# One core, two branches (dilated attention and a long convolution): even and odd tokens instead of mirrored ones, partner frequencies by adding DMAs, and an order written by a planner

## The chip, the cores and the metric

The kernel runs on one core of a Trainium2 chip. Its engines are TensorE (PE, with a queue of weight loads, PEld), VectorE (DVE), ScalarE (ACT), GpSimd (POOL) and SyncE (SP, which here only issues DMAs). Each engine has a queue of its own that it works through in order; sixteen DMA engines serve all of them. The metric is the device time of one execution in microseconds. Three runs of the kernel before took 237.39, 239.34 and 239.98 us.

## The reference

Two independent branches over 2048 tokens with 576 channels (bf16), written side by side into an output of 2048 x 1152.

```python
# A: attention in 32 heads of 18 channels; each token sees itself and 7 earlier ones, 2 apart
qkv = x @ wqkv
logits = einsum("bhsd,bhswd->bhsw", q, kg) * 18 ** -0.5   # kg, vg: k, v at pos - 2 * (0..7)
o = einsum("bhsw,bhswd->bhsd", softmax(mask(logits)), vg)
a = o @ wo
# B: a causal 4-tap filter on k, gated by v, then a convolution as long as the sequence
kv = (sum over t of k[s - 3 + t] * shift_k[:, 3 - t]) * v
y = irfft(rfft(pad(kv, 2 * S)) * rfft(pad(ssm_k, 2 * S)))[:S] + kv * ssm_D
b = q * y
```

## The kernel before

**Branch B.** The convolution is cut into 4 blocks of 512 tokens. Each block i of kv is turned into a spectrum by matmuls with tables of sines and cosines (`x_spectrum`, in PSUM `ps_fx`, stored in `xw`), each block m of the filter likewise (`filter_spectrum`, `ps_fk`, stored in `Ks`). Output block j is the sum over i of spectrum i times filter spectrum j-i (`products` on DVE, L757, and `sums` on PE, L777, which adds the terms by matmuls with `ident` and `identn` in `ps_z`), turned back by `inverse` (`ps_inv`), multiplied by q and stored (`gate`).

The kv block itself is made by `taps` on DVE (L417 to L421): four products with shifted k, three sums and the product with v, from `kj` and `vt`, each in two buffers. `mirror` (L430 to L437) then reverses half of each block by matmuls with `flip`, copies it twice by ACT, and two adding DMAs from POOL's queue form sums and differences of mirrored tokens; the x spectrum needs two table steps instead of four. The filter is not mirrored: a unit of `filter_spectrum` runs four steps (`c`) of 128 tokens, each a pair of matmuls with 384 and 192 columns (L454, L455), and there are 8 units in each of 4 blocks. `turn_filter` (L477) then adds neighbouring filter spectra by six adding DMAs. `inverse` computes one half of the tokens as `A` and `y`, and `back` (L810) makes the mirrored half from them by `flip2` and `flipn`.

The tables are made by DVE in integers (L328 to L330: two scalings and a wrap of the period per table call) and by ACT with a sine (L331): four calls for the filter's table `TK` and two for `TX`, whose period is twice as long.

**Branch A.** x is transposed (partly by PE, `ps_x`, partly by DMA transposes from SP, L167), then `project` makes q, k (both in `qk`) and v. `logits` (L550 on DVE, L559 on PE) multiplies q by eight shifted copies of k and sums over each head's 18 channels with the 0/1 matrices `E`. `hh` is 0 or 1 and takes 256 tokens of every 512. `softmax` is on DVE with one exponential on ACT (L583). `spread` (L626) copies the weights of 32 partitions over X by four DMAs from SP; `weigh` (L648, L664, L675) multiplies X by shifted v and sums over the eight positions on PE (`ps_acc`). `output` (L702, L705) is the product with wo, stored from ACT's queue (L714).

**Memory that is used twice.** `xw` holds the three projection weights and the transposed x, and later the x spectra. `Ks` holds x as it comes and the integer tables, later the filter's spectra. `qk` holds q and k, later X, products and wo. kj, vt and the weights of the taps are in a pool that is closed before v and the softmax weights get their place.

**The order.** DVE's work is written out in program order. PE's units wait in a list, `units`; after certain DVE steps `until` takes as many of them as the next number in `PLACES` says (66 numbers), and `need` takes all units up to a label. Two estimates of time per engine (`clk`) are only used to choose among units and to place the gates. PSUM is two double banks with tag A and two with tag B.

## Time and profile before

| | |
|---|---|
| runs | 237.39, 239.34, 239.98 us; median 239.34 |
| span of the profiled execution, first to last instruction | 239.0 us |
| that span against the median of the runs | 0.34 us less |
| mean granted TensorE clock | 0.984 |
| matmuls, DVE, ACT, POOL instructions | 2032, 152, 213, 61 |
| DMA | 33.75 MB, 29559 packets; HBM read 13.11 MB, written 4.72 MB |

The profile is of one execution. It gives each engine's busy time; a chain of work that ended last, followed back from the last instruction; groups of equal instructions with their mean time and what ended the idle time before them; and the DMAs with the time from issue to landing. A line such as `L757 DVE TENSOR_TENSOR qk<-xw,Ks 128x3072 ... x30 | 50.7, 1752 | 2.2 <-PE ps_z` reads: line 757 of the kernel, on DVE, output and inputs, shape, 30 times; 50.7 us in all, 1752 ns each; 2.2 us of idle time before them, most of it ended by PE's work on `ps_z`. Matmuls are pipelined, so the durations of single matmuls overlap.

### The profile page before, as it was taken

The page shows a single profiled execution, that of the slowest core. Times are in us where ns is not written, and L with a number is a line of the kernel's source. Part 1 is how long each engine was busy: PE and PEld are TensorE (multiplying, and loading weights), DVE is VectorE, ACT ScalarE, POOL GpSimd, SP SyncE. Part 2 cuts the span into 40 slices and gives each one's busy share as a digit, 9 for nine tenths or more (in the row PEclk, how much of TensorE's full clock was granted, in tenths as well). Part 3 has the DMA queues.
Part 4 walks back from the last instruction along what each step waited for, and adds up shares of the span by engine and source line. Part 5 has one row for each costly group of instructions (what it writes and reads, how often), then busy time and mean ns, then how long its engine had stood idle before and what let it go on. Part 6 is the DMA issues. An engine that isn't in the chain of part 4 may idle for free.

```text
span 239.0 us, 4802 instructions
## 1 busy us (share of the span) xinstructions
PE 219.5 (92%) x2032; PEld 116.5 (49%) x2041; DVE 206.0 (86%) x152; ACT 156.7 (66%) x213; POOL 28.9 (12%) x61
## 2 busy tenths in 40 slices
PE   4899998999899999999998976989999999999991
PEld 2533443345545566533343443445555666666550
DVE  7599999999898896989899593889997899999931
ACT  6796778579965568565585575454568766736551
POOL 8600010202120000402108100000000000000000
PEclk9999999999999999999999999799999999999996
DMA  6999999999541000299975999907203102323233
GB/s 198 309 224 326 247 289 148 352 154 199 105 81 22 0 0 3 38 164 225 188 137 99 129 265 251 265 21 247 76 27 101 51 3 101 99 101 101 99 103 99
DMA packets 29559, 33.75 MB, mean 141 GB/s; under 512 B 16577, under 2 KB 23617, under 8 KB 29537
## 3 DMA queue, kind: packets, MB, share of 16 engines
q1 hardware_dynamic: 23712, 22.08, 38.0%
q0 software_dynamic: 3648, 9.00, 19.1%
q10 hardware_dynamic: 2176, 2.36, 2.9%
q8 instruction: 16, 0.26, 0.5%
q14 instruction: 7, 0.05, 0.1%
HBM read 13.11 MB, written 4.72 MB: 75 GB/s over the span
## 4 chain that ended last, share of the span: by engine, by line
PE 58%; DVE 21%; ACT 9%; SPq 5%; DMA 3%; issue 2%; DVEq 0%
PE ps_z L777 9%; PE ps_fk L454 8%; PE ps_wo L702 7%; PE ps_inv L799 7%; PE ps_proj L284 6%; SPq L626 5%; PE ps_log L559 4%; PE ps_fk L455 4%; DVE ab L420 3%; DVE tB L417 3%; PE ps_acc L664 3%; DMA X<-attn 3%; PE ps_acc L675 2%; DVE qk L648 2%; PE ps_back L810 2%
## 5 line engine op out<-in xcount | busy, mean ns | idle before, releaser
L757 DVE TENSOR_TENSOR qk<-xw,Ks 128x3072 bf16<-128x3072 bf16 x30 | 50.7, 1752 | 2.2 <-PE ps_z L777 2.0
L284 PE MATMUL ps_proj<-xw 128*128 128x512 bf16 x183 | 47.4, 385 | 2.2 <-ACT v L306 1.0
L550 DVE TENSOR_TENSOR prod<-qk 128x4096 bf16<-128x4096 bf16 (+1 forms) x20 | 40.6, 2074 | 4.3 <-PE ps_log L559 3.9
L454 PE MATMUL ps_fk<-kTok,TK 128*128 128x384 bf16 x128 | 32.6, 327 | 0.4 <-ACT qk L306 0.2
L455 PE MATMUL ps_fk<-kTok,TK 128*128 128x192 bf16 x128 | 31.4, 246 | 0.0
L284 PEld LDWEIGHTS <-xw 128*128 128x128 bf16 x192 | 17.1, 99 | 23.4 <-issue 8.6
L466 ACT ACTIVATE Ks<-ps_fk 128x576 bf16<-128x576 f32 x32 | 20.6, 651 | 12.0 <-PE ps_fk L455 11.9
L518 ACT ACTIVATE xw<-ps_fx 128x576 bf16<-128x576 f32 x32 | 19.9, 649 | 7.5 <-PE ps_fx L455 7.3
L306 ACT ACTIVATE qk<-ps_proj 128x1024 bf16<-128x1024 f32 x18 | 18.6, 1035 | 8.7 <-PE ps_proj L297 8.5
L784 ACT ACTIVATE Yall<-ps_z 128x768 bf16<-128x768 f32 x24 | 18.1, 810 | 4.4 <-PE ps_z L777 4.4
L454 PE MATMUL ps_fx<-ab,TX 128*128 128x384 bf16 x64 | 18.2, 332 | 1.8 <-ACT xw L518 1.7
L799 PE MATMUL ps_inv<-Yall,TI 128*128 128x288 bf16 (+2 forms) x128 | 19.0, 287 | 0.6 <-ACT yA L811 0.6
L702 PE MATMUL ps_wo<-qk,pv 128*128 128x288 bf16 x128 | 18.4, 287 | 0.6 <-ACT xw L518 0.6
L454 PEld LDWEIGHTS <-TK 128*128 128x128 bf16 x128 | 12.5, 98 | 12.4 <-issue 5.0
L803 ACT ACTIVATE yA<-ps_inv 128x576 bf16<-128x576 f32 (+2 forms) x16 | 10.4, 652 | 10.9 <-PE ps_inv L802 7.1
L777 PE MATMUL ps_z<-qk,ident 64*64 64x384 bf16 x288 | 16.7, 326 | 0.0
L420 DVE TENSOR_TENSOR ab<-ab,tB 128x2304 bf16<-128x2304 bf16 x12 | 16.3, 1358 | 0.4
L417 DVE TENSOR_TENSOR tB<-kj,skb 128x2304 bf16<-128x2304 bf16 x12 | 16.3, 1356 | 0.3
L648 DVE TENSOR_TENSOR P<-X,v 128x4096 bf16<-128x4096 bf16 x6 | 13.6, 2288 | 2.7 <-DMA X<-attn 1.2
L664 PE MATMUL ps_acc<-P,ident 64*64 64x512 bf16 x192 | 15.7, 379 | 0.3 <-DVE P L648 0.3
L455 PE MATMUL ps_fx<-ab,TX 128*128 128x192 bf16 x64 | 15.8, 247 | 0.0
L799 PEld LDWEIGHTS <-TI 128*128 128x128 bf16 x128 | 11.4, 98 | 6.8 <-issue 3.8
(126 smaller groups left out, 349.0 us busy)
## 6 DMA issues: line engine op xcount, KB each, us to landing
Ks<-Ks POOLq DMA_DIRECT2D x6, 576.0 KB, 11.5
qk<-attn SPq DMA_DIRECT2D x12, 256.0 KB, 7.0
kj<-in_B_k_dram SPq DMA_DIRECT2D x3, 1008.0 KB, 6.4
vt<-in_B_v_dram SPq DMA_DIRECT2D x4, 576.0 KB, 6.0
qB<-in_B_q_dram POOLq DMA_DIRECT2D x4, 576.0 KB, 4.1
out_dram<-qk ACTq DMA_DIRECT2D x8, 288.0 KB, 2.4
X<-attn SPq DMA_DIRECT2D x8, 256.0 KB, 9.4
out_dram<-qB SPq DMA_DIRECT2D x3, 576.0 KB, 4.8
```

The source lines that it names most:

```text
L284: nc.tensor.matmul(ps[:, jp, :], wq(kb, comp, 128 * ct, 128), xT(kb, 1024 * jj + 512 * jp, 512), start=(kb == 0), stop=False)
L417: dve(2304, lambda: nc.vector.tensor_tensor(o, kj[:, 3 - j:7 - j, :], skb[:, j, :].unsqueeze(1).to_broadcast([128, 4, D]), ALU.mult))
L420: dve(2304, lambda: nc.vector.tensor_tensor(kv, kv, o, ALU.add))
L454: nc.tensor.matmul(o[:, 0:2, :], w, rhs[:, 0:2, :], start=start, stop=stop)
L455: nc.tensor.matmul(o[:, 2, :], w, rhs[:, 2, :], start=start, stop=stop)
L466: nc.scalar.activation(Ks[:, 3 - m, cs, :, gi, :], acc3(ps), ACT.Copy, scale=(CSG, SSG)[cs][m] * 2.0 / 1024.0)
L550: r = dve(1024 * nj, lambda: nc.vector.tensor_tensor(view(prod, 0, [[256 * nj, 4], [256, nj], [1, 256]]), view(t, o + 256 * hh, [[0, 4], [ ...
L664: nc.tensor.matmul(acc[64 * o:64 * o + 64, h, :], ident[64 * h:64 * h + 64, 64 * h:64 * h + 64], view(P, 256 * u, [[2048, 2], [1, 256]])[6 ...
L702: nc.tensor.matmul(ps[:, r, 0:HD], oT(hh, j + 2 * r, t)[:, o:o + 128], wo[:, t // 2, t % 2, HD * h:HD * h + HD], start=(t == 0), stop=False)
L757: r = dve(3072, lambda: nc.vector.tensor_tensor(pr, view(xw, i * SPB + 4 * TH * t, [[4 * D, 2], [0, 2], [1, 4 * TH]]), view(Ks, (3 - j + i ...
L777: nc.tensor.matmul(acc[r][o:o + 64, h, 0:2 * TH], w[64 * h:64 * h + 64, 64 * h:64 * h + 64], pr[64 * h:64 * h + 64, part, cs, 2 * TH * s:2 ...
L799: nc.tensor.matmul(ps[:, c, 0:n], TI[:, sl, pm, 128 * c:128 * c + 128], Yall[:, j % 2, pm, sl, c0:c0 + n], start=(sl == 0), stop=(pm == 0 ...
```

## The change

The whole program is rewritten on the same tiling of the work.

- **Even and odd tokens.** There is no `mirror`, `flip` or `back`. One sine table `T` (period 2048, 256 frequencies per token class) serves the x spectra, and, copied by four DMAs into `tabk`, the filter. A unit (`pair`) computes the even tokens' sum first, and ACT stores it times -2 at the place of a partner frequency; then the odd tokens' sum is added in the same PSUM bank and stored at the frequency itself. `partners` adds the second to the first by one adding DMA for each block, 6 runs of 384 elements in each partition, 576 KB in all, on `Ks` for the four filter blocks and on `xw` for the four x blocks. The filter's spectrum has 4 units a block in place of 8, of four pairs of matmuls each as before; the x spectrum has 4 in place of 8, of four pairs in place of two.
- **The inverse** takes two evictions per piece and no matmul from `yA`. `sums` uses one double bank with two passes; `fold` adds one pass's result to the other, by an adding DMA for output blocks 0 to 2 and on DVE for block 3.
- **Filter loads.** A filter block is transposed by DMA into a stage in `Ks`, and four DMAs from POOL's queue split it into even and odd rows of `kTok`.
- **Halves of 1024 tokens.** `hh` now means tokens 0 to 1023 and 1024 to 2047, in logits, softmax, weighing and output.
- **The order.** Every piece of work is given to `Plan.op` with its engine, an estimate of its time, what it reads and writes, and the PSUM bank it opens or closes. `Plan.emit` builds one static order for all engines from these estimates: DVE, the loads on SP by program order (DVE may look ahead by 0.8 us), PE and ACT by the longest path to the end. PSUM is four double banks shared by all uses.
- **Queues.** The q blocks are loaded and all outputs stored from SP; seven places are used in turn for the spectrum products in place of four.

```diff
...
+    SLOTS = 4
+    HOP = 0.15
+    PATIENCE = 0.8
...
+    def op(self, eng, us, fn, r=(), w=(), opens=None, closes=None, mode=None, lat=0.0, bus=0.0, chain=False, bias=0.0):
...
+    def emit(self):
...
+                s = min(cand)[0]
+                now = [n for t, n in cand if t <= s + 1e-6]
+                if e in ("S", "G"):
+                    n = min(now)
+                elif e == "D":
+                    t, n = min((c for c in cand if c[0] <= s + self.PATIENCE), key=lambda c: c[1])
+                    s = t
+                elif e == "P":
+                    n = max(now, key=lambda n: (level[n] + (0.6 if ops[n]["mode"] == mode else 0.0), -n))
+                else:
+                    n = max(now, key=lambda n: (level[n], -n))
+                if best is None or s < best[0]:
+                    best = (s, e, n)
...
+    def table(c):
+        def ts(cs):
+            nc.vector.tensor_scalar(n_all[:, c, cs, :], fr_i, rp[:, c:c + 1], float(512 * (1 - cs)), op0=ALU.mult, op1=ALU.add)
+        for cs in range(2):
+            op("D", 0.35, partial(ts, cs), w=[reg("Ks", 2 * SPB + 1024 * c + 512 * cs, 512)], chain=True)
...
+    def wrap(c):
+        rg = [reg("Ks", 2 * SPB + 1024 * c, 2048)]
+        op("D", 1.15, lambda: nc.vector.tensor_single_scalar(n_all[:, c:c + 2], n_all[:, c:c + 2], 2047, ALU.bitwise_and),
+           r=rg, w=rg, chain=True)
+        op("A", 1.05, lambda: nc.scalar.activation(T[:, c:c + 2], n_all[:, c:c + 2], ACT.Sin, bias=pib[:],
+                                                   scale=-2.0 * np.pi / 2048), r=rg, w=[reg("T", 512 * c, 1024)])
...
+    def load_filter(m):
+        at = stage_at[m]
+        stage = view(Ks, at, [[D, 4], [1, D]])
+        load(0.75, lambda: nc.sync.dma_start_transpose(stage, B_ssm_k[:, BL * m:BL * m + BL]),
+             [reg("Ks", at, 4 * D)])
+
+        def part():
+            for par in range(2):
+                for h in range(2):
+                    nc.gpsimd.dma_start(kTok[64 * h:64 * h + 64, m, :, par], view(stage, h * D, [[2 * D, 2], [1, D]])[par::2])
+        op("G", 4.0, part, r=[reg("Ks", at, 4 * D)], w=[reg("pv", 4 * D * m, 4 * D)], bus=3.0, lat=3.0)
...
+    load_x(0)
+    load_w(0, wv[:, 0], [r_w(0)])
+    load_x(1)
+    load_k(0)
+    load_w(1, wv[:, 1], [r_w(1)])
+    load_v(0)
+    turn_x(0)
+    load_k(1)
+    load_v(1)
...
+    def table_k():
+        for e in range(2):
+            for b in range(2):
+                nc.gpsimd.dma_start(view(TK, 1024 * e, [[1, 1024]])[b::2],
+                                    T[64 * e:64 * e + 64, 2 * b:2 * b + 2].rearrange("p c s f -> p (c s f)"))
+    op("G", 4.0, table_k, r=[reg("T", 0, 2048)], w=[reg("tabk", 0, 4096)], bus=1.0, lat=2.5)
...
-    def table(n_i, T, vec, col, period, off0, off1):
-        nc.vector.tensor_scalar(n_i[:, 0, :], vec, rp[:, col:col + 1], float(off0), op0=ALU.mult, op1=ALU.add)
-        nc.vector.tensor_scalar(n_i[:, 1, :], vec, rp[:, col:col + 1], float(off1), op0=ALU.mult, op1=ALU.add)
-        nc.vector.tensor_single_scalar(n_i, n_i, period - 1, ALU.bitwise_and)
-        nc.scalar.activation(T, n_i, ACT.Sin, bias=pib[:], scale=-2.0 * np.pi / period)
-
-    def table_k(c):
-        table(n_all[:, 2 * c:2 * c + 2, :], TK[:, c, :, :], n_all[:, 8, :], c, 2048, 512, 0)
...
-    def table_x(c):
-        table(n_all[:, 2 * c:2 * c + 2, :], TX[:, c, :, :], n_all[:, 8, :], 4 + c, 4096, 512, 1536)
...
-    def mirror(i):
...
-        for c in range(2):
-            for h in range(2):
-                nc.tensor.matmul(ps[c][:, h, 0:HD], flip[:], b[:, 1 - c, HD * h:HD * h + HD], start=True, stop=True)
-            nc.scalar.activation(halves(kr[:, c, :]), ps[c][:, :, 0:HD], ACT.Copy)
-            pe(0.25, "B", 0.65, last=False)
-        for c in range(2):
-            nc.scalar.activation(halves(b[:, c, :]), ps[c][:, :, 0:HD], ACT.Copy, scale=-1.0)
-            pe(0.0, "B", 0.65, first=False)
-        nc.gpsimd.dma_start(b, a, accum_op=ALU.add)
-        nc.gpsimd.dma_start(a, kr, accum_op=ALU.add)
-
...
+    def pair(key, name, mms, dst, scale, r, base, tile_name):
+
+        own = reg(str(key), 0, 1)
+        for step in range(2):
+            def mm(step=step):
+                if step == 0:
+                    bank2(key, name)
+                mms(step)
+            op("P", 0.5, mm, r=r, w=[own], opens=key if step == 0 else None, mode="f")
+
+            def ev(step=step):
+                nc.scalar.activation(dst(step), acc3(banks[key]), ACT.Copy, scale=scale * (1.0 if step else -2.0))
+            op("A", 0.65, ev, r=[own], w=[own] + [reg(tile_name, base(step) + 4 * TH * t, TH) for t in range(3)],
+               closes=key if step else None)
...
+    def partners(t, base, name):
+
+        op("G", 1.0, lambda: nc.gpsimd.dma_start(view(t, base + 2 * TH, [[4 * TH, 6], [1, 2 * TH]]),
+                                                 view(t, base, [[4 * TH, 6], [1, 2 * TH]]), accum_op=ALU.add,
+                                                 max_dma_last_dim=768),
+           r=[reg(name, base, SPB)], w=[reg(name, base, SPB)], bus=3.0, lat=7.0,
+           bias=30.0 if name == "Ks" else 0.0)
...
     def filter_spectrum(m):
-        def unit(gi, cs):
-            ps = bank2("ps_fk", "A")
-            skip = m == 0 and cs == 0
-            for c in range(4):
-                mm3(ps, TK[:, c, cs, 128 * gi:128 * gi + 128], thirds(kTok[:, m, c, :]), c == 0, c == 3 and not skip)
...
+        for gi in range(2):
             for cs in range(2):
-                units.append((1.0, partial(unit, gi, cs), "fk"))
+                def mms(par, gi=gi, cs=cs):
+                    skip = par == 0 and m == 0 and cs == 0
+                    for e in range(2):
+                        mm3(banks[("fk", m, gi, cs)], TK[:, e, par, cs, 128 * gi:128 * gi + 128],
+                            thirds(kTok[:, m, e, par, :]), par == 0 and e == 0, e == 1 and not skip)
+                    if skip:
...
+        partners(Ks, (3 - m) * SPB, "Ks")
...
+    def x_spectrum(i):
+        for gi in range(2):
             for cs in range(2):
...
+                def mms(par, gi=gi, cs=cs):
+                    for n, c in enumerate((par, par + 2)):
+                        mm3(banks[("fx", i, gi, cs)], T[:, c, cs, 128 * gi:128 * gi + 128], thirds(ab[:, i, c, :]),
+                            par == 0 and n == 0, n == 1)
...
+        taps(i)
         if i < 2:
             load_k(i + 2)
             load_v(i + 2)
...
+            turn_x(1)
+            load_filter(0)
...
+            load_w(2, wraw, [reg("big", o_wraw, 5 * D)])
+            for m in range(1, NBL):
+                load_filter(m)
...
+    RING = [(qk, "qk", 0), (qk, "qk", 3072), (big, "big", 8 * D), (qk, "qk", 6144), (qk, "qk", 9216),
+            (big, "big", PR[0]), (big, "big", PR[1])]
+    JORD = (0, 1, 2, 3)
...
-    def load_q(j):
...
+        j = JORD[n]
+        qB = view(t, o, [[D, 4], [1, D]])
+        op("S", 0.06, lambda: nc.sync.dma_start(qB, qf[BL * j:BL * j + BL, :].rearrange("(p c) d -> p c d", c=4)),
...
-        def back():
-            ps = bank2("ps_back", "A")
-            for c in range(2):
-                for src, w in ((A, flip2), (y, flipn)):
-                    nc.tensor.matmul(ps[:, c, 0:n], w[:], src[:, 1 - c], start=(src is A), stop=(src is y))
-            nc.scalar.activation(y[:, 2:4], ps[:, :, 0:n], ACT.Copy)
...
+    def sums(n, j, t, prs):
+        key = ("z", j, t)
+        own = reg("z", 4 * j + t, 1)
+        for q in range(2):
...
+                        bank2(key, "ps_z")
+                    z = banks[key]
+                    sc, ss = CSG[j - i], SSG[j - i]
+                    for k, terms in enumerate((((0, 0, sc), (0, 1, ss)), ((1, 1, -ss), (1, 0, sc)))):
+                        for r, (part, cs, sign) in enumerate(terms):
+                            w = ident if sign > 0 else identn
+                            for h in range(2):
+                                o = 64 * ((h + r) % 2)
+                                nc.tensor.matmul(z[o:o + 64, h, 0:2 * TH], w[64 * h:64 * h + 64, 64 * h:64 * h + 64],
+                                                 pr[64 * h:64 * h + 64, part, cs, 2 * TH * q:2 * TH * q + 2 * TH],
+                                                 start=(q == 0 and i == 0 and k == 0), stop=(i == j and k == 1), skip_group_check=True,
+                                                 tile_position=(64 * h, o))
+                op("P", 0.37, mm, r=[rpr], w=[own], opens=key if q == 0 and i == 0 else None, mode="q")
+
+            def ev(q=q):
+                nc.scalar.activation(view(y_at(n, 1 - q, t, TH), 0, [[2 * D, 2], [D, 2], [1, TH]]),
+                                     view(banks[key], 0, [[512, 2], [TH, 2], [1, TH]]), ACT.Copy, scale=(-2.0, 1.0)[q])
+            op("A", 0.81, ev, r=[own], w=[own] + ry(n, 1 - q, t), closes=key if q else None)
...
+    def fold(n, t0, t1):
+
+        rr = [x for t in range(t0, t1) for x in ry(n, 0, t)]
+        ww = [x for t in range(t0, t1) for x in ry(n, 1, t)]
+        u, d = y_at(n, 0, t0, TH * (t1 - t0)), y_at(n, 1, t0, TH * (t1 - t0))
+        if t1 - t0 == 3:
+            op("G", 1.0, lambda: nc.gpsimd.dma_start(y_at(n, 1, 0, 4 * D)[:, 0], y_at(n, 0, 0, 4 * D)[:, 0], accum_op=ALU.add,
+                                                     max_dma_last_dim=2304), r=rr + ww, w=ww, bus=3.0, lat=7.0)
+        else:
+            op("D", tt_us(4 * TH * (t1 - t0)), lambda: nc.vector.tensor_tensor(d, d, u, ALU.add), r=rr + ww, w=ww, chain=True)
...
+    def inverse(n, c0, w):
+        ts = range(c0 // TH, (c0 + w - 1) // TH + 1)
+        y = yA[:, n % 2, :, c0:c0 + w]
+        for par in range(2):
+            key = ("inv", n, par, c0)
+            own = reg(str(key), 0, 1)
+
+            def mm(par=par, key=key):
+                ps = bank2(key, "ps_inv")
+                for c in range(2):
+                    for s in range(4):
+                        nc.tensor.matmul(ps[:, c, 0:w], TI[:, s // 2, s % 2, 2 * c + par, :],
+                                         Yall[:, n % 2, par, s // 2, s % 2, c0:c0 + w], start=(s == 0), stop=(s == 3))
...
+    for n, j in enumerate(JORD):
+        for t in range(3):
+            sums(n, j, t, [products(j, t, i) for i in range(j + 1)])
+            if n == 3 and t:
+                fold(n, 0 if t == 1 else 2, t + 1)
+                inverse(n, 0 if t == 1 else 2 * TH, 2 * TH if t == 1 else TH)
+            if n and t == 2 and n < 3:
+                gate(n - 1, 0, D)
+                load_q(n + 1)
+        if n < 3:
+            fold(n, 0, 3)
+            inverse(n, 0, HD)
+            inverse(n, HD, HD)
+    gate(2, 0, D)
...
```

More of the change, by code (lines that the diff above doesn't have):

```diff
@@ L571, in softmax @@
+            yield
+    uses = []
+    def softmax(hh, tmp, rtmp):
+        at, ra = attn[hh], reg("big", AT[hh], 2048)
         t4 = view(tmp, 0, [[256, 4], [1, 256]])
@@ L671, in weigh @@
             P, r = product(4)
-            until()
-            acc = bank2("ps_acc", "B")
-            for u in range(W):
-                nc.tensor.matmul(acc[:, 0, :], ident[:], view(P, 256 * u, [[2048, 2], [1, 256]]),
-                                 start=(u == 0), stop=(u == W - 1))
-            pe(1.75, "B", 0.6, r)
-            nc.scalar.activation(view(pv, 4608 * hh + 4096, [[1, 512]]), acc[:, 0, :], ACT.Copy)
-            yield
+            key = ("acc", n, 0)
+            own = reg("acc", 10 * n, 1)
@@ new lines, in mm @@
+            def mm():
+                acc = bank2(key, "ps_acc")
+                for u in range(W):
+                    nc.tensor.matmul(acc[:, 0, :], ident[:], view(P, 256 * u, [[2048, 2], [1, 256]]),
+                                     start=(u == 0), stop=(u == W - 1))
+            op("P", 1.75, mm, r=[r], w=[own], opens=key, mode="f")
+            at = 4608 * hh + 4096
+            op("A", 0.6, lambda: nc.scalar.activation(view(pv, at, [[1, 512]]), banks[key][:, 0, :], ACT.Copy),
+               r=[own], w=[reg("pv", at, 512)], closes=key)
```

1076 lines of the change are left out of this document (571 added, 505 removed).

## The prediction

> **What bounds the kernel now.** I read the page's busy times first, then the chain that ended last, then a table of five stretches that follow the code (tables and taps, logits, weighing of v, spectrum products, end), and last the waits of DVE.
>
> ```profile
> PE 219.5 (92%) x2032; PEld 116.5 (49%) x2041; DVE 206.0 (86%) x152; ACT 156.7 (66%) x213; POOL 28.9 (12%) x61
> PE 58%; DVE 21%; ACT 9%; SPq 5%; DMA 3%; issue 2%; DVEq 0%
> ```
>
> Two engines are nearly full. PE carries the chain, but DVE has only 33.0 us of idle in a span of 239.0, so no relief of PE can save more than that. The stretches show where it lies (columns: length, then busy time and instruction count of PE, weight load, DVE, ACT, POOL; then granted clock, DMA share and GB/s):
>
> ```profile
> 0.00:60.00 60.00, 53.89 (x322) 24.14 (x327) 54.57 (x58) 45.94 (x57) 13.08 (x40) 1.00 1.07 245
> 60.00:115.00 55.00, 53.49 (x465) 29.19 (x466) 48.00 (x32) 36.06 (x51) 7.65 (x9) 1.00 0.40 74
> 115.00:172.00 57.00, 50.88 (x474) 25.60 (x472) 47.76 (x29) 34.45 (x47) 7.07 (x10) 0.97 0.75 168
> 172.00:227.00 55.00, 55.00 (x707) 33.50 (x697) 52.83 (x32) 35.90 (x53) 1.06 (x2) 1.00 0.23 77
> 227.00:239.00 12.00, 6.28 (x82) 4.05 (x80) 2.88 (x4) 4.39 (x7) 0.00 (x0) 0.83 0.31 100
> ```
>
> DVE idles 5.4, 7.0, 9.2, 2.2 and 9.1 us in them. The waits of DVE name who ended the idle time:
>
> ```profile
> DVE qB L820 <- ACT yA L811: 5.6, 2, 3.9
> DVE prod L550 <- PE ps_log L559: 3.9, 5, 1.2
> DVE qk L648 <- DMA X<-attn: 3.4, 1, 3.4
> DVE xw L358 <- PE ps_x L356: 3.3, 4, 1.4
> DVE qk L648 <- PE ps_acc L664: 3.1, 2, 2.7
> DVE qk L757 <- PE ps_z L777: 2.0, 2, 1.6
> ```
>
> The 8 us of PE waits in the logits, weighing and product stretches (ps_log, ps_acc, ps_z) are what a lighter PE can give back. The DMA waits need a freer queue.
>
> **The change, part by part**, against the profiled execution's span of 239.0.
>
> *PE in all.* Durations of single matmuls overlap, so I take pitches. A pair of 384 and 192 columns starts every 0.245 us in the timeline, so a filter unit of four pairs takes 0.98 and 32 units 31.3 us; 16 units of the same size take 15.7: -15.7. The x spectra keep their columns (16 units of four pairs for 32 of two). In the inverse, per piece of 288 columns, the mirrored half costs 0.49 (the ident matmuls, 1.58 against 1.09 in the chain) and 0.60 (back); over six pieces and the last two about 8.2 go. Flips: four times 0.65, 2.6. PE falls by some 26 us to 193. ACT loses the 16 flip evictions (9.5), 8 of back (5.1) and four table calls (4.5). DVE stays at about 201 (below), so DVE becomes the bound, and only its idle time counts.
>
> *Tables and taps (0 to 60).*
>
> ```profile
> L330 DVE TENSOR_SCALAR Ks<-Ks 128x1024 int32<-128x1024 int32 x6 | 4.2, 694 | 0.2
> L328 DVE TENSOR_SCALAR Ks<-Ks,rp 128x512 int32<-128x512 int32 x6 | 2.9, 489 | 0.1
> L329 DVE TENSOR_SCALAR Ks<-Ks,rp 128x512 int32<-128x512 int32 x6 | 2.9, 488 | 0.0
> ```
>
> These 10.0 us become two wraps of 1024 (1.4) and eight scalings of 256 columns. No row has that form; it lies between the 6-column cast (0.11) and the 512-column row (0.49), and I take the 256-column cast, 0.29, so 2.3. DVE is free 6.3 earlier, but the taps, which start at 16.35, need kj: its pieces are issued from 4.3 to 6.1 behind the same loads as before and land after 7.5 to 8.2, so at 13.3. The gain is 3.0 at most. Block 1's kj is issued at 16.3 behind a DMA transpose that holds SP 5.1 us, and loads of kj land after 5.6 to 11.0: at 21.9 to 27.3, wanted at 13.3 + 10.9 = 24.2. With a DMA share of 1.07 nothing in this stretch comes early. I take **-2.5**, bounds 0 and -3.
>
> The flips' cover was PE time beside the taps; their two adding DMAs a block leave POOL as well. In their place POOL gets the splitting of each filter block (four DMAs, 0.85 to 1.6 us each by the rows of POOL DMAs, so 14 to 26 us in all), beside taps and logits, where POOL is 13 to 22% busy.
>
> *Logits (60 to 115).* PE is 97% full there, 30 of its 53 us with the filter's spectrum. Half of that goes; the first logits need only the first 1024 tokens of q and k, so ten of the twenty projection units can come later. Each new unit waits for an eviction between its even and odd half, so the filter costs ACT 32 x 0.65 = 20.8 us and is ACT's more than PE's; ACT has 19 us idle here. Of the 7.0 idle, the 1.9 for the softmax's exponential stays, with one E group at the end of each set. I take **-4**, bounds 0 and -6.
>
> *Weighing of v (115 to 172).* PE waits of 4.0 and X waits of 4.6 make up the idle.
>
> ```profile
> Ks<-Ks POOLq DMA_DIRECT2D x6, 576.0 KB, 11.5
> qk<-attn SPq DMA_DIRECT2D x12, 256.0 KB, 7.0
> ab<-ab POOLq DMA_DIRECT2D x4, 288.0 KB, 9.4
> ```
>
> The columns end in KB and median us to landing. The six Ks<-Ks adds start at 98.6, 111.9 and 126.5, just where SP spreads attn over X, and the DMA share is about 1.0. With the filter done earlier they move out of the spreads' way, and wo's load with them. Against that stand four new adds of 576 KB on xw: they wait for the x spectra, which overwrite the projections' weights and x and so cannot come before the v projections (about 100). Four on Ks come before, and the three folds later, where the DMA share is 0.23. As 2.3 MB of adds leave this stretch and 2.4 come in, the X waits may stay; the PE waits should go. I take **-3**, bounds +4 and -7.
>
> *Products (172 to 227).* PE is 55.00 of 55.00 busy and DVE waits 2.0 for ps_z. With 7 us less of back and ident, PE leaves that bound: -2.2. The last block's first fold comes to DVE (1536 columns as in the gate: 0.96): +1.0. The second accumulation of z waits for the eviction of the first (0.81), with seven product buffers in place of four; nothing queued is late. **-1.2**, bounds +1 and -2.2. q's loads and wo's stores move to SP, whose last waits are for DVE anyway.
>
> *End (227 to 239).* Now 12.0 us from the last product. After: last z half 0.39, eviction 0.81, four second halves 1.55, eviction 0.81, fold 0.56, inverse 0.65, eviction 0.50, gate 0.56, store and finish 3.5 (as now from 235.5), and 0.8 for eight hand-overs: 10.1. **-1.9**, bounds 0 and -3.
>
> Sum: -2.5 - 4 - 3 - 1.2 - 1.9 = -12.6, span 226.4. The shown runs have a median of 239.34, 0.34 above that span, so I forecast **227 us**; the parts' bounds reach from 218 to 244.
>
> **A rule against the change.** Between 145 and 150 PE is busy 2.74 of 5 us, and in the next 5 us the granted clock is 0.70. The Trainium skill, "TensorE: Matmul & The Clock Gate", section "Why this matters for your kernels", says to allow no idle gap of PE over about 3 us, since the clock then falls back. The trace agrees with it. A lighter PE has more such gaps; by that rule two more would cost PE 0.3 x 5 = 1.5 us each, and the sum would be 229 to 230 if DVE waited for all of it.
>
> **The rivals.**
>
> *The adding DMAs come late (slower).* POOL works in order. A partner add moves 576 KB like Ks<-Ks, but in 768 runs a DMA in place of 128. The Ks<-Ks row has 1.4 us of POOL each; if the cost goes by runs it is 8.5. At 1.4, the chain from the end of the filter (95): one landing of 11.5 and three turns of 12 each, done near 142, the xw adds between. At 8.5, eight adds put 57 us on top, to 199, and the products, due at 160, wait for xw's first block. It decides once that add lands after 160. Half of the spread, 20 us late: 247. For it: POOL waited 23.0 us on its own Ks<-Ks adds. Against: POOL has 88% free and the DMA share is 0.18 or less from 70 to 100. The Trainium skill, "SBUF — State Buffer", describes in its box on the "DVE blocks DMA" trap that POOL cannot write descriptors while DVE runs some of its modes. Here POOL's adds took 0.85 to 1.4 us while DVE was 98% busy, so the trace does not bear out a lasting block.
>
> *The written order waits in the wrong place.* The plan counts 0.06 us of SP for a load; the traces show transposes that hold SP 3.5 to 14.7 us, and a filter block now has a second hop behind it. If PE's queue has a filter unit ahead of an E group, DVE, with two product buffers, stops with it; two waits of 8 us eat the gain: 236 to 246.
>
> *DVE alone counts.* If PE waits only change their names, the gain is the taps' start, the end and little more: 233 to 236.
>
> **How the numbers follow.** A change of 1% (2.4 us) is about what a measurement of this kernel can tell from none. Forecast (218 to 233) 0.48; DVE alone 0.12; late adds 0.18; order 0.22, of which 0.06 falls within 1% (237 to 241.7). So faster 0.60, same 0.06, slower 0.34. The likeliest sign's own range is 218 to 236; to hold 8 in 10 the range must take in the order's waits and the nearer half of the late adds: 217 to 250.
>
> **What would show it.** PE busy 190 to 197, DVE 199 to 203, ACT near 138; first tap at 13 to 14 us; no wait of DVE over 1 us for ps_log or ps_z; X waits of 2 to 5 us; the last product 10 us before the end. I am wrong if the first spectrum products wait for a DMA on xw or Ks, if PE stands before filter units for kTok, or if the taps stop for kj by more than 3 us.

## The result and the profile after

| | before | after |
|---|---|---|
| median of the runs, us | 238.51 (237.39 to 239.98) | 248.44 (247.13 to 249.37) |
| profiled execution: time, span, us | 239.34, 239.0 | 249.37, 247.7 |
| ratio after to before | | 1.0409, 95% interval 1.0324 to 1.0494 |

The kernel became 4% slower. Forecast were 227 us and a faster kernel; the range to 250 holds the time, the sign is wrong. Some executions of a kernel fall into a slower state; medians and ratios here and below are of the executions outside it, while the expectations, written ahead of their runs, quote medians of all (235.83 us for 234.69, and 11.8 us for 11.4). The lines of the page of the kernel after that answer to the two shown of before (busy time of each engine, and who holds the chain that ended last):

```profile
PE 203.3 (82%) x1838; PEld 102.9 (42%) x1845; DVE 201.0 (81%) x144; ACT 136.2 (55%) x186; POOL 45.4 (18%) x74
...
PE 44%; DMA 17%; DVE 17%; issue 10%; ACT 7%; SPq 3%; POOL 0%; DVEq 0%; ACTq 0%; POOLq 0%
```

PE lost 16.2 us of work and DVE 5.0, as meant. The chain shows where they went: DMA holds 17% of it, against 3% before. The same five stretches of the kernel after (length, then busy time and count of PE, weight load, DVE, ACT, POOL; then granted clock, DMA share, GB/s):

```profile
0.00:60.00 60.00, 52.03 (x298) 22.38 (x304) 50.88 (x49) 36.62 (x41) 16.61 (x45) 1.00 0.98 253
60.00:115.00 55.00, 53.57 (x441) 25.52 (x442) 50.70 (x37) 39.78 (x60) 18.43 (x21) 1.00 0.87 138
115.00:172.00 57.00, 38.79 (x341) 20.75 (x343) 33.41 (x19) 22.64 (x34) 6.75 (x5) 0.82 0.95 180
172.00:227.00 55.00, 45.99 (x612) 26.59 (x606) 54.11 (x32) 30.17 (x42) 3.59 (x3) 1.00 0.45 118
227.00:248.00 21.00, 12.97 (x152) 7.66 (x151) 11.86 (x10) 7.03 (x10) 0.00 (x0) 0.87 0.17 57
```

All of the loss is in the third row. DVE is busy 33.41 of its 57 us (47.76 before) and the DMA share is 0.95 (0.75 before). Cut by DVE's own milestones instead of fixed times (first product of the logits, first of the weighing, first and last product of the spectra):

| stage | before | after | difference | forecast |
|---|---|---|---|---|
| start to first logits product | 60.15 | 58.05 | -2.1 | -2.5 |
| logits | 55.0 | 51.7 | -3.3 | -4 |
| weighing of v | 56.7 | 71.4 | **+14.7** | -3 |
| products of the spectra | 55.2 | 54.9 | -0.3 | -1.2 |
| last product to the end | 12.0 | 11.6 | -0.4 | -1.9 |

The differences make +8.6, and the spans differ by 8.7. DVE's waits in the kernel after (what was waited for: total us, times, longest):

```profile
DVE big L797 <- DMA tabk<-big: 15.8, 1, 15.8
...
DVE qk L797 <- DMA pv<-big: 4.5, 1, 4.5
DVE big L707 <- PE ps_log L717: 3.4, 2, 2.6
...
DVE ab L988 <- ACT ab L975: 2.7, 2, 2.1
DVE qk L797 <- PE ps_acc L817: 2.3, 2, 1.8
```

Two waits for the spread weights of the softmax (chunk 3's, in `X` before and in `tabk` now, and chunk 2's, in `pv`) make 20.3 us. Before they made 4.6: the 3.4 us that the forecast shows, and

```profile
DVE P L648 <- DMA X<-attn: 1.2, 1, 1.2
```

The chain that ended last, in order of time, tells what they stood behind (start us, us, what):

```profile
104.62 6.24 DMA qk<-in_A_wo_dram
...
111.48 14.80 DMA xw<-xw
...
126.37 2.62 SPq L773
...
129.09 10.88 DMA pv<-big
...
148.32 9.76 DMA tabk<-big
```

It runs through the load of wo, the first of the new partner adds on xw, and then through SP's spreads of chunks 2 (`pv`) and 3 (`tabk`). POOL's queue in the same time (start us, us, engine, line, operation, tiles):

```profile
107.11 0.62 POOL L851 DMA_DIRECT2D qk<-in_A_wo_dram  x1 [1.85 <-DVE big L707]
...
109.96 2.51 POOL L638 DMA_DIRECT2D Ks<-Ks  x2
111.48 2.47 POOL L611 DMA_DIRECT2D xw<-xw  x1
118.62 1.43 POOL L611 DMA_DIRECT2D xw<-xw  x1 [4.67 <-ACT xw L605]
124.44 1.43 POOL L611 DMA_DIRECT2D xw<-xw  x1 [4.39 <-ACT xw L605]
125.35 2.96 POOL L638 DMA_DIRECT2D Ks<-Ks  x2
128.79 1.45 POOL L611 DMA_DIRECT2D xw<-xw  x1 [0.48 <-ACT xw L605]
```

The turn adds (`Ks<-Ks`, L638) were to move out of the spreads' way. The second pair starts at 109.96 and the third at 125.35. Before, they were hardly later:

```profile
111.91 2.44 POOL L477 DMA_DIRECT2D Ks<-Ks  x2 [10.85 <-DMA Ks<-Ks]
126.47 2.44 POOL L477 DMA_DIRECT2D Ks<-Ks  x2 [12.12 <-DMA Ks<-Ks]
```

The second now stood in POOL's queue behind wo's load, which waits for DVE's logits. The four partner adds came on top. And SP's queue, after and then before:

```profile
124.03 7.19 SPq L773 DMA_DIRECT2D pv<-big  x4
131.35 9.23 SPq L773 DMA_DIRECT2D qk<-big  x4
141.12 9.70 SPq L773 DMA_DIRECT2D tabk<-big  x4
150.91 6.94 SPq L773 DMA_DIRECT2D qk<-big  x4
```

```profile
129.42 5.20 SPq L626 DMA_DIRECT2D pv<-attn  x4
134.72 7.76 SPq L626 DMA_DIRECT2D X<-attn  x4
142.52 9.75 SPq L626 DMA_DIRECT2D qk<-attn  x8
```

DVE weighs in the order of chunks 2 (`pv`), 3 (`tabk`), 4 and 5 (`qk`). The planner's order spreads chunk 4 ahead of chunk 3, although the program names chunk 3 first; before, SP issued `pv`, X for chunk 3, then both `qk`. A spread holds SP's queue for 7 to 10 us in the kernel after. So there were two suspects: the bytes of the adds, and the order of the spreads. A third, TensorE's own written order, came up on the way.

### The profile page after: what moved, and what is told of

It is laid out like the page before. It is cut to its first block, busy times and chain, and to the rows that moved or that the text cites. A ratio compares the mean times of both kernels' runs of the same rounds, so it can differ in the third digit from the quotient of the medians.

```text
span 247.7 us, 4427 instructions
## 1 busy us (share of the span) xinstructions
PE 203.3 (82%) x1838; PEld 102.9 (42%) x1845; DVE 201.0 (81%) x144; ACT 136.2 (55%) x186; POOL 45.4 (18%) x74
## 3 DMA queue, kind: packets, MB, share of 16 engines
q0 software_dynamic: 9968, 13.65, 35.0%
## 4 chain that ended last, share of the span: by engine, by line
PE 44%; DMA 17%; DVE 17%; issue 10%; ACT 7%; SPq 3%; POOL 0%; DVEq 0%; ACTq 0%; POOLq 0%
PE ps_proj L492 13%; PE ps_z L968 7%; PE ps_inv L1001 6%; DMA xw<-xw 6%; DVE big L707 5%; DMA pv<-big 4%; DMA tabk<-big 4%; PE ps_wo L869 4%; SPq L773 3%; DVE qk L941 3%; PE ps_fk L591 3%; DMA qk<-in_A_wo_dram 3%; PE ps_acc L817 2%; PE ps_proj L497 2%; DVE qk L797 2%
## 5 line engine op out<-in xcount | busy, mean ns | idle before, releaser
L707 DVE TENSOR_TENSOR big<-qk 128x4096 bf16<-128x4096 bf16 (+1 forms) x20 | 40.3, 2073 | 4.0 <-PE ps_log L717 3.4
L941 DVE TENSOR_TENSOR qk<-xw,Ks 128x3072 bf16<-128x3072 bf16 x18 | 30.9, 1750 | 0.0
L817 PE MATMUL ps_acc<-big,ident 64*64 64x512 bf16 x192 | 19.7, 442 | 12.9 <-DVE big L797 10.7
L797 DVE TENSOR_TENSOR big<-tabk,big 128x4096 bf16<-128x4096 bf16 x6 | 13.6, 2287 | 16.9 <-DMA tabk<-big 15.8
L975 ACT ACTIVATE ab<-ps_z 128x768 bf16<-128x768 f32 x24 | 18.9, 808 | 13.3 <-PE ps_z L968 13.2
L824 ACT ACTIVATE pv<-ps_acc 128x1024 bf16<-128x1024 f32 x8 | 8.2, 1023 | 30.6 <-PE ps_acc L817 30.6
L516 ACT ACTIVATE qk<-ps_proj 128x1024 bf16<-128x1024 f32 x16 | 15.7, 1024 | 14.5 <-PE ps_proj L497 14.5
L941 DVE TENSOR_TENSOR big<-xw,Ks 128x3072 bf16<-128x3072 bf16 x12 | 20.7, 1749 | 0.0
L817 PEld LDWEIGHTS <-ident 64*64 64x64 bf16 x256 | 9.3, 117 | 26.4 <-issue 16.3
L1001 PE MATMUL ps_inv<-ab,TI 128*128 128x288 bf16 (+2 forms) x128 | 18.2, 293 | 0.9 <-ACT ab L975 0.9
L591 PE MATMUL ps_fk<-pv,tabk 128*128 128x384 bf16 x64 | 16.8, 328 | 0.2 <-ACT Ks L605 0.2
L572 DVE TENSOR_TENSOR ab<-ab,big 128x2304 bf16<-128x2304 bf16 x12 | 16.3, 1358 | 0.4
L591 PE MATMUL ps_fx<-ab,T 128*128 128x384 bf16 x64 | 16.6, 326 | 0.0
L569 DVE TENSOR_TENSOR big<-big 128x2304 bf16<-128x2304 bf16 x12 | 16.3, 1355 | 0.3
```

Source lines behind the costliest of these rows:

```text
L569: nc.vector.tensor_tensor(o, kj[:, 3 - j:7 - j, :], skb[:, j, :].unsqueeze(1).to_broadcast([128, 4, D]), ALU.mult)
L591: nc.tensor.matmul(o[:, 0:2, :], w, rhs[:, 0:2, :], start=start, stop=stop, skip_group_check=True)
L707: nc.vector.tensor_tensor(view(prod, 0, [[m, 4], [1, m]]), view(t, oq, [[0, 4], [1, m]]), view(tk, oo + 2 + 8 * ug, [[2, 4], [1, m]]), ALU ...
L797: op("D", tt_us(4096), lambda: nc.vector.tensor_tensor(view(P, 0, [[2048, 2], [256, W], [1, 256]]), view(X, xo, [[2048, 2], [256, W], [1, ...
L817: nc.tensor.matmul(acc[64 * o:64 * o + 64, h, :], ident[64 * h:64 * h + 64, 64 * h:64 * h + 64], view(P, 256 * u, [[2048, 2], [1, 256]])[6 ...
L941: op("D", 1.752, lambda: nc.vector.tensor_tensor(pr, view(xw, i * SPB + 4 * TH * t, [[4 * D, 2], [0, 2], [1, 4 * TH]]), view(Ks, (3 - j + ...
```

## The experiments

Each kernel was timed beside the kernel before. Ratios are to it, with their 95% intervals; "from after" is the difference of medians to 248.44. All variants of the kernel after keep the four partner adds on `Ks`.

| kernel | median us | ratio | from after |
|---|---|---|---|
| spread of chunk 3 first | 244.11 | 1.0247 (1.0206 to 1.0289) | -4.3 |
| no xw adds | 237.02 | 0.9909 (0.9867 to 0.9950) | -11.4 |
| both | 235.47 | 0.9886 (0.9839 to 0.9932) | -13.0 |
| both, no turn adds either | 233.38 | 0.9745 (0.9686 to 0.9804) | -15.1 |
| xw adds in longer runs | 247.20 | 1.0337 (1.0277 to 1.0398) | -1.2 |
| chunk 3 first, xw adds held back | 234.69 | 0.9836 (0.9771 to 0.9901) | -13.8 |
| the same, replanned | 233.23 | 0.9766 (0.9718 to 0.9815) | -15.2 |
| replanned, wo behind the turns | 236.28 | 0.9896 (0.9859 to 0.9933) | -12.2 |
| replanned, no xw adds and no turn adds | 229.14 | 0.9561 (0.9515 to 0.9608) | -19.3 |
| before, chunk 4 spread first | 245.21 | 1.0270 (1.0196 to 1.0344) | |
| before, no turn adds | 237.11 | 0.9930 (0.9885 to 0.9976) | |

### The order of the spreads

```diff
         line = [n for _, _, n in self.order]
+        late, soon = self.spreads[4], self.spreads[3]
+        line.remove(late)
+        line.insert(line.index(soon) + 1, late)
```

> The changed kernel, with only the order of two steps on SP's queue exchanged: the four DMAs that spread the weights for chunk 3 are issued before those for chunk 4, as in the kernel before; every other engine's order is as in the changed kernel. Theory (the written order of SP's queue makes the loss): chunk 3's X, issued at 131 in place of 141, lands near 148 in place of 158; DVE's wait of 15.8 us for it falls to 5 to 7, the next X may add 1 or 2, and the kernel takes 239 to 242 us. Rival (the DMA engines are full between 130 and 160, so that the order only chooses who waits): the wait moves to chunk 4, the sum of the waits for X falls by less than 4, and the time stays at 245 to 249.

244.11 us, 4.3 less, between the two ranges. The waits of DVE for the spreads in the profiled execution (241.58 us, the fastest of four):

```profile
DVE big L804 <- DMA tabk<-big: 6.8, 1, 6.8
DVE qk L804 <- DMA pv<-big: 4.7, 1, 4.7
```

The wait for chunk 3 fell from 15.8 to 6.8, the one for chunk 2 stayed. So the order is one cause; the next experiment shows a larger one. The same swap was made in the kernel before, where no partner adds exist:

```diff
-    spread(3)
...
     spread(4)
+    spread(3)
```

> The kernel before, with the spreads for chunk 4 issued ahead of those for chunk 3, as the changed kernel has it. Theory of the order: chunk 3's X lands 7 to 10 us later, DVE waits for it that long, and the kernel takes 245 to 249 us. Rival (the order does not matter by itself): 238 to 241.

245.21 us, 6.7 more than before. In the profiled execution (242.80 us, again the fastest) its wait for chunk 3 is `DVE P L648 <- DMA X<-attn: 5.9, 1, 5.9`, against 1.2. One swap of two issues on SP's queue costs the old kernel 2.7%. What made the planner choose the new order was not tried; it counts 4.0 us of bus for a spread that holds SP for 7 to 10.

### The partner adds on xw

```diff
-        op("G", 1.0, lambda: nc.gpsimd.dma_start(view(t, base + 2 * TH, [[4 * TH, 6], [1, 2 * TH]]),
+        op("G", 1.0, lambda: name == "xw" or nc.gpsimd.dma_start(view(t, base + 2 * TH, [[4 * TH, 6], [1, 2 * TH]]),
```

> The changed kernel without the four adding DMAs on xw (the partner half of the x spectra is left unfinished, so the convolution's output is not the reference's); the order of all queues is otherwise as in the changed kernel. Theory of the order: the waits for X shrink by the DMA time of 2.3 MB spread over the stretch, 3 to 5 us, to 244 to 246. Rival (the adds take the DMA engines from the spreads): the wait for pv's X (4.5) goes and the wait for chunk 3's X falls from 15.8 to 8 or less: 236 to 240.

237.02 us, 11.4 less: in the rival's range, and 0.9% under the kernel before in place of 4% above it. With SP's order as in the kernel after, the waits for the spreads shrink from 15.8 and 4.5 us to

```profile
DVE big L797 <- DMA tabk<-big: 7.2, 1, 7.2
...
DVE qk L797 <- DMA pv<-big: 3.1, 1, 3.1
```

The second was to go and stayed in part. With the spreads' order changed too:

> Both edits together (the partner half of the x spectra is left unfinished). If the two causes add up, the gains of the two single runs come together: 232 to 237. If one hides the other, it is no better than the better of the two by more than 1.5 us.

235.47 us, 13.0 less. The two causes overlap: 4.3 and 11.4 alone, 13.0 together. Against the kernel that only leaves out the adds the intervals overlap, so what the order is worth once they are gone is not settled. What is left of DVE's waits in that stretch:

```profile
DVE big L804 <- PE ps_acc L824: 4.7, 2, 3.8
...
DVE big L804 <- DMA tabk<-big: 2.5, 1, 2.5
DVE qk L804 <- DMA pv<-big: 2.1, 1, 2.1
```

What the adds take of the DMA engines can be read from the queue of POOL, in the kernel after and then in the one without these adds (packets, MB, share of 16 engines):

```profile
q0 software_dynamic: 9968, 13.65, 35.0%
```

```profile
q0 software_dynamic: 6832, 11.29, 28.3%
```

0.350 x 247.7 x 16 - 0.283 x 235.8 x 16 = 320 engine-us for 2.36 MB, or 20 us of all sixteen, in a stretch of 57 us whose DMA share was 0.75 before. These times include what a packet waits beside others, so 320 is an upper reading; the packets' own records in the trace of the kernel after give 93 ns on average for the 768-byte packets of this queue, and 284 engine-us for the 3072 that belong to these adds. The Trainium skill, "DMA: Bandwidth & Descriptors", section "Specifications", gives about 27 GiB/s for one DMA engine; by that 2.36 MB would be 81 engine-us, an estimate from the page, 5 us of all. The runs show three and a half to four times as much for these adding DMAs.

Are the short runs of memory to blame (384 elements, 768 bytes)? The same bytes in runs of 1152 elements:

```diff
-        op("G", 1.0, lambda: nc.gpsimd.dma_start(view(t, base + 2 * TH, [[4 * TH, 6], [1, 2 * TH]]),
...
+        to, src = view(t, base + 2 * TH, [[4 * TH, 6], [1, 2 * TH]]), view(t, base, [[4 * TH, 6], [1, 2 * TH]])
+        if name == "xw":
+            to, src = view(t, base + 4 * D, [[1, 4 * D]]), view(t, base, [[1, 4 * D]])
+        op("G", 1.0, lambda: nc.gpsimd.dma_start(to, src, accum_op=ALU.add, max_dma_last_dim=2304 if name == "xw" else 768),
```

> The changed kernel, in which each of the four adds on xw moves the same 576 KB between the same two halves of a block's bytes, but in 2 runs of 1152 elements in each partition in place of 6 of 384 (it adds the sine part to the cosine part, so the convolution's output is not the reference's). Theory (an add costs the DMA engines by its runs): the four adds took 319 engine-us (the difference of the POOL queue's share with and without them), or 20 us of all sixteen; the long runs, at the 81 engine-us per MB of the kernel before, take 190, or 12 us. Eight of the twenty us go, and of the 11.8 us that the adds cost in all some 4 to 5: 243 to 246. Rival (they cost by their bytes, or by holding POOL's queue): 247 to 250.

247.20 us, in the rival's range. POOL's queue has 7920 packets for the same 13.65 MB at 33.2%, so 0.332 x 245.8 x 16 - 1068 = 238 engine-us, a quarter less. But the wait for chunk 3 stays, 16.3 us for 15.8 (`DVE big L798 <- DMA tabk<-big: 16.3, 1, 16.3`), and the 1.2 us that the kernel gains lie within the intervals. So the short runs do cost the DMA engines time, but most of the loss does not come from them. Whether the bytes as such cost it or the moment at which they move, the held adds below tell.

### No xw adds and no turn adds

The kernel without xw adds, chunk 3 first, and the loop of the turn adds emptied (`for cs in range(0)`); the partner adds on `Ks` remain:

> Spreads in the order of the kernel before, no adds on xw, and none of the six adds that turn the filter's spectra (3.5 MB; the convolution's output is not the reference's). Theory (what is left of the miss in the weighing stretch is DMA time too): the waits for X that remain without the xw adds, 4.6 us in the profile, go, and the kernel takes 229 to 232 us, near the forecast of 227. Rival (the rest is PE's order: ps_acc waits of 4.7 us): 234 to 236, as without the xw adds alone.

233.38 us, between the two ranges, and less than with the turn adds: by 2.1 us in the medians, by 3.4 in the ratios to the kernel before. No wait for a spread is left; in its place stands TensorE:

```profile
DVE big L804 <- PE ps_acc L824: 7.0, 2, 6.3
```

The wait for `ps_acc`, which frees DVE's product buffers, grew from 4.7 to 7.0 when the transfers went. PE's instructions are written in the planned order, with seven output products (`ps_wo`) ahead of chunk 3's accumulation; that order was made for a chunk 3 that comes after chunk 4. When X comes early, PE is in the wrong place. This was not in the forecast.

### Holding the adds back

The adds are needed only when the products of the spectra begin. So they can wait behind the spreads, all work done:

```diff
+        for n in self.held:
+            line.remove(n)
+        at = max(line.index(d) for d in [late] + [d for n in self.held for d in ops[n]["deps"]]) + 1
+        line[at:at] = [self.gate] + sorted(self.held)
...
+    held = main.tile([128, 1], BF16, name="held")
+    plan.hold = lambda: nc.gpsimd.tensor_copy(held[:], view(qk, 4096 + 2048, [[1, 1]]))
```

A copy of one element per partition of chunk 4's X holds POOL's queue until that spread has landed.

> All work is done, with the spreads in the order of the kernel before and the four adds on xw held back: a small copy on POOL reads the X of chunk 4 and so waits until it has landed, and the adds follow it. Theory (the adds hurt only by the stretch in which they run; the DMA share is 0.29 to 0.52 from 160 to 180): X comes as early as without them, the adds land between 155 and 172, and the products, due at 167, wait 0 to 3 us for the first block: 235 to 239, below the kernel before or level with it. Rival (the products then wait for the adds, as POOL issues them one after the other): 242 to 247.

234.69 us. The four adds, moved, cost nothing that these runs can tell: the kernel that has none of them took 235.47, and the intervals overlap. With all the work done, this kernel is 1.6% faster than the kernel before. So it is the stretch in which the adds run that costs, and not their bytes as such. Then the spreads' order was given to the planner instead of being changed behind it, so that PE and ACT are planned for it too:

```diff
-        op("S", 0.24, fn, r=[reg("big", AT[hh], 2048)], w=[reg(name, o, 4096)], bus=4.0, lat=3.0)
+        plan.spreads[n] = op("S", 0.24, fn, r=[reg("big", AT[hh], 2048)], w=[reg(name, o, 4096)] + ([reg("ord", 0, 1)] if n in (3, 4) else []), bus=4.0, lat=3.0)
```

> All the work is done, as in the kernel with the held adds (235.83 us): the four adding DMAs of the spectra of x wait behind chunk 4's X. The difference is in the plan: a dependency makes the spread of chunk 3 come ahead of chunk 4's already when the order of the instructions is planned, so that TensorE's and ScalarE's written orders follow it too (three output products, then the accumulation, instead of seven output products ahead of chunk 3's accumulation). Theory: the 4 to 7 us that VectorE still waited for the accumulation's product in the runs with SyncE's order changed by hand is TensorE's written order; replanned, that wait falls under 2 us and the time is 231 to 234 us. Rival: TensorE is late there for other reasons (its clock, the taps behind DMAs), the order of output products matters nothing: 235 to 237 us, and the wait stays at 4 us or more, for the accumulation or for another tile.

233.23 us, the fastest version that does the whole computation, 2.3% under the kernel before (1.9 to 2.8). The third row of its stretches and DVE's waits there:

```profile
115.00:172.00 57.00, 46.81 (x474) 25.48 (x475) 49.30 (x28) 29.73 (x44) 10.53 (x7) 0.94 0.98 192
```

```profile
DVE big L808 <- PE ps_wo L880: 3.9, 1, 3.9
...
DVE qk L808 <- PE ps_acc L828: 2.1, 1, 2.1
DVE big L808 <- DMA qk<-big: 1.2, 1, 1.2
```

DVE is busy 49.30 of 57 us where it was 33.41. The DMA share is 0.98, higher than in the kernel after: the same traffic, but the four adds on xw, which start at 157.12, no longer run beside the spreads that DVE wants next. The time met the theory; of the waits half came true, since 3.9 us behind PE remained, now behind `ps_wo`. Against the kernel with the adds held but not replanned the intervals overlap, so here the gain of replanning is not settled.

### wo's load behind the turns

```diff
+        line.remove(self.wo)
+        line.insert(line.index(self.turn) + 1, self.wo)
```

> The replanned kernel with the held adds, and the load of wo issued behind the filter's turn adds on GpSimd's queue instead of ahead of the second one, where it waited from 104.6 to 109.4 us for VectorE's logits. Theory: the second and third turn adds go out some 8 to 13 us earlier and their bytes leave the time of the spreads for chunks 3 and 4; the wait for pv and X shrinks by 1 to 2 us, and so does the time. Rival: the load of wo lands in their place and the sum of bytes in that stretch is the same: within 1 us of the replanned kernel.

236.28 us, 3.1 more, outside both ranges: the theory was wrong in sign. The second and third pair of turn adds went out at 105.91 and 120.67, only 4 to 5 us earlier than in the replanned kernel (111.01, 124.92), since each pair also waits for the one before it to land. The load of wo went from 105.7 to 122.1, into the spread of chunk 2:

```profile
DVE qk L810 <- DMA pv<-big: 6.3, 1, 6.3
```

That wait was 0.3 us in the replanned kernel; the median landing of `pv` went from 8.7 to 13.8 us. Its old place, which I had blamed for holding up the turns, was the better one.

### What remains of the adds, and the price of the turns before

> The replanned kernel (spread of chunk 3 ahead of chunk 4's in the plan) without the four adding DMAs of the spectra of x and without the six turn adds of the filter: the partner halves of x's spectra stay unfinished and the turned blocks of the filter are left out of the sum. Its counterpart is the kernel with SyncE's order changed by hand and no adds (233.38 us). Theory: with these DMAs gone only the written order of TensorE was left between that kernel and the forecast, so it comes to 228 to 231 us, with no wait of VectorE over 3 us between its logits and its products. Rival: held adds and turn adds cost the replanned kernel (233.23 us) nothing, since DMA has room where they go: 232 to 234 us.

229.14 us, in the expected range. DVE's waits in this kernel's weighing:

```profile
DVE big L808 <- PE ps_acc L828: 2.4, 2, 1.3
...
DVE qk L808 <- PE ps_acc L828: 1.8, 2, 1.3
```

Against its counterpart whose PE order was left alone (233.38) it gains 4.2 us, and the intervals are apart. In the traces DVE and SP work through the same list in both; PE's and ACT's lists differ around chunk 3 alone, and POOL has the one small copy more. So that is the price of the written order of PE and ACT once X comes early. Against the replanned kernel with all adds (233.23) it gains 4.1: the four held adds and the six turn adds together still cost that. Its weighing of v takes 51.9 us, 4.8 less than before, where the forecast had 3 less.

> The kernel before, without its six turn adds of the filter (the turned blocks are left out of the sum), and nothing else changed. It prices the step of the forecast by which moving these adds out of the time of the spreads would have given some 3 us in the weighing of v. Theory of the forecast: 1.5 to 4 us faster than before, since the wait for the pair of X is shorter. Rival: they cost the kernel before nothing that shows (within 1 us), because TensorE's own work is late behind the same tiles.

237.11 us, a gain of 1.6 us in the medians and of 1.7 (0.6 to 2.7) by the ratio: the lower end of the expected range. In the profiled executions the weighing of v is 4.1 us shorter (52.6 for 56.7), but that of the kernel before was a slower one (239.34). The 3.4 us wait for X on chunk 2 and the one of 1.2 on chunk 3 are gone from this kernel; beside the latter the wait for `ps_acc` grew from 0.9 to 1.4.

## Why the prediction was wrong

**The step that failed is the weighing of v**, -3 with bounds +4 and -7; it measured +14.7, and the other four terms together came to -6.1 for -9.6. Inside it:

- "With the filter done earlier they move out of the spreads' way, and wo's load with them." The turn adds did not: two and three started 2.0 and 1.1 us earlier than before. I had freed them of the filter, and not followed what else stands ahead of them on POOL: each other's landing, and wo's load behind DVE's logits, which did move (from 127.93 to 104.62) and now stood in front. Had the step come true, it would have been worth some 1.7 us, by the kernel before without turns.
- "As 2.3 MB of adds leave this stretch and 2.4 come in, the X waits may stay." As the turn adds did not leave, 2.4 MB came on top of a stretch with a share of 0.75 to 1.0. The X waits went from 4.6 to 20.3 us. Taking the adds out gives back 11.4 us; with SP's spreads in the order of the kernel before, moving them behind the spreads gives back as much as taking them out (244.11 to 234.69, and to 235.47). The bound of +4 had no mechanism behind it; a stretch near a share of 1.0 with 20 us more of DMA had one.
- The order of the spreads on SP appears in no step. It cost 4.3 us here and 6.7 in the kernel before. The change was "planned order", and I read the plan's costs for loads, and not the order in which it issues the four spreads against the order in which DVE wants them.
- "The PE waits should go." In the kernel after they were 3.4 us for `ps_acc` in this stage, hardly less than the 4.0 before; with X early they were up to 9.1, and replanning PE and ACT then gained 4.2 us.

**The rivals.** The adding DMAs did decide, and the rival's 247 us lies near the time, but by luck and not by its mechanism: POOL took 1.4 to 2.5 us for each, not 8.5, and no product of the spectra waited for xw. They were not late but early, in the way of others. The written order as a rival was right in kind and in the size of a wait (two waits, 236 to 246), but I had placed it on the filter units; it was SP's order around chunk 3, and PE's only once X came early. The three signs by which the forecast was to be known wrong all stayed away: no product waited for xw or Ks, PE did not wait for kTok, and the taps did not stop for kj. None of them looked at the spreads.

**The clock rule.** Where the kernel after leaves PE idle, between 130 and 145, PE is busy 7.58 of 15 us and the granted clock there is 0.72. So idle time and a lower clock go together again, but "The trace agrees with it" was too strong for the about 3 us that the forecast quotes from the Trainium skill. In the kernel before the clock falls to 0.50 at 149.6, right behind an idle stretch of 2.26 us (146.95 to 149.21), the longest there. In the kernel after it falls at 136.6, and no idle stretch of PE in the 40 us ahead of that is longer than 2.26 us either. So shorter gaps came ahead of a fall here. The lower clock is no rival for the loss: in the kernel after DVE waits 3.4 us for PE in this stage and 20.3 for the spreads. In the replanned kernel without xw and turn adds the clock is still 0.91 there, and DVE waits 4.2 us for PE in all.

**The other terms.** Tables and taps, -2.1 for -2.5, and the logits, -3.3 for -4, were right within a microsecond, but in part by luck. The taps began at 14.27, not at the landing of kj, which DVE no longer had to wait for, but behind a copy of the transposed x, for which it waited 6.6 us on PE. In the logits the 1.9 us for the exponential, which were to stay, went, and the waits for ps_log, which were to go, stayed (3.4 us for 3.9). Products gave -0.3 for -1.2: the PE bound left as forecast (45.99 of 55 us busy), but two new waits for ACT of 0.6 us each, ahead of the gate and of the last fold, were not counted. The end gave -0.4 for -1.9: the inverse of the last piece takes 1.49 us (16 matmuls), where I put 0.65, and the second half of z stands behind 2.72 us of inverse on PE. DVE at 201.0 and ACT at 136.2 were as forecast; PE's 203.3 was 10 over. The PE waits that the forecast put at 8 us make 9.0 in the lines that it shows; the sum does not use them.

The forecast's sum was thus within reach of this design (span 227.2 without the xw and turn adds, 226.4 forecast), but not with its work done: 233.23 is the best that was shown.

## What to carry to other kernels

When a change trades engine work for DMA, put the new bytes into the stretch where they will be issued, add them to the DMA share that the stretch already has, and ask which transfer of that stretch an engine waits for; an average share over the kernel says nothing. Of each queue, compare the order of issue with the order in which the consumer wants the data: two swapped spreads were worth 4 to 7 us, and holding back transfers that nobody wants yet was worth more. When a wait is removed, look at the written order of the next engine behind it, since a plan made for the late arrival keeps its place.

## What the runs showed of the hardware

- Adding DMAs from SBUF to SBUF occupied the DMA engines for about 100 to 135 engine-us per MB, waiting included (238 and 320 engine-us for 2.36 MB, in runs of 2304 and 768 bytes). Those on xw landed 11.7 to 29.5 us after issue in the full stretch of the kernel after.
- Transfers that POOL issued delayed transfers that SP issued: the adds on xw, and the load of wo where it stood beside the spread of chunk 2. The Trainium skill, "DMA: Bandwidth & Descriptors", section "Issuing engines are not separate DMA queues", says that all of them share the same sixteen engines and interleave; the landing of `pv` at 8.7 us, and at 13.8 with wo's load beside it, agrees.
- A DMA share of 0.95 and one of 0.98 went with 33.41 and 49.30 us of DVE work in the same 57 us: the share alone does not tell whether DMA is the bound.
